# A list scheduler's delays, durations and engine hold replaced by measured ones: sliding-window attention and a two-layer expert on one Trainium2 core

## Chip, core and metric

One core of one Trainium2 chip. The metric is device time in microseconds (us) of one execution; the median of runs is given. Engines: PE is TensorE, DVE is VectorE, ACT is ScalarE, POOL is GpSimd, SP is SyncE (here it issues nearly all DMAs).

## The reference

Sliding-window attention over 8 sequences of 576 tokens with 8 heads of 64, then a two-layer network with a squared ReLU over all 4608 tokens:

```python
scores = scale * np.matmul(q, k.transpose(0, 1, 3, 2))        # q, k, v: (8, 8, 576, 64)
mask = np.abs(pos[:, None] - pos[None, :]) <= 32
attn = softmax(np.where(mask, scores, -1e9))
x = (attn @ v).transpose(0, 2, 1, 3).reshape(4608, 512)
h = np.maximum(x @ w_in, 0.0)                                 # w_in: (512, 2048)
out = (s * (h * h) + b) @ w_out                               # w_out: (2048, 512), out float32
```

Inputs and output are float32; the kernel multiplies in bfloat16.

## The kernel before

**A graph and a planner.** The kernel does not write its instructions in order. It calls `add` (L95) for each task: the engine ("stream"), the instructions, a cost in ns, the tiles read and written, and a key, which is a due time. `plan` (L126) then plays all engines forward: each engine has a time from which it is free, each task a time from which its inputs are ready, and the task that can start first is taken next, ties going to the lower key (L191 to L208). `release` (L175) sets when a user of a finished task is ready: its end, plus 100 ns for a DMA, 60 ns on the same engine, or the producer's `LAT` (L86), and 250 ns of `MARGIN` (L87) more where the user is PE. DMA rings have a model of their own (`serve`, `space`). `emit` (L234) writes each engine's tasks in the planned order with semaphore waits. On the chip every engine executes its own list strictly in order; so the plan's times decide nothing but the order, and where that order is wrong an engine waits in front of one task while a later one could run.

**Opening (sequence 0).** Q and K are loaded by pairs of heads, cast to bfloat16, transposed on PE (L704), evicted (L709 ACT for Q, L710 DVE for K), multiplied into scores (L943, into banks opened by L961), and passed through the exponential (L986 ACT). V is loaded by rows, cast (L602), placed by matmuls (L620) and evicted (L629, L630). Then each of five units is done: attention times V in 64-row tiles of PE (L868), reciprocal (L892) and product (L894) on DVE, a transpose on PE (L901) and a copy on ACT (L909) into the expert's input `xt`. The rest of sequence 0 beyond 512 tokens goes through L719 and L972.

**Expert.** The first layer (`s1`, matmuls L1123) works on a block of tokens (224, 128, 160, 256, 256, then 512 each) and a group of the 16 hidden tiles, into one of two banks `W`; ACT takes the ReLU (L1130), DVE squares (L1132). The second layer (`s2`, L1141; for the first three blocks `early`, L1172) accumulates 16 matmuls of 512 columns into a bank; DVE scales and adds (L1157), SP stores. Weights are loaded in eight pieces a layer and cast on POOL (L556). The pieces of the second layer hold their users back in the plan by `HELD` (L38) in place of `LAT`. `colsum` (L1182 to L1191) forms the column sums of the second weight.

**Later sequences.** Sequence 1 is turned on PE as sequence 0 is; from sequence 2 on, K and Q are cast on POOL (L759), transposed by DMA, and K is rearranged on POOL (L776). A unit there is one PE task (`pe_part`, L923): the first half of attention times V (L868), the scores of another unit (L810), and the second half, all in 64-row tiles between full-array matmuls. Its cost in the plan is a constant `SWITCH` plus 230 for scores plus 340 for attention times V. Exponential (L838 ACT) and mask (L842 DVE) follow, and V is cast on DVE (L590). Keys: the opening's PE tasks have keys from -99 to -21, the first blocks of the expert from -20 on, sequence 1 from -17.5 on.

Of the kernel before, what the change touches and what calls it, by code (L numbers as in the profile page):

```python
# [41 lines left out]
SWITCH = 215.0  # L42
# [23 lines left out]
class _Task:  # L66
    __slots__ = ("n", "stream", "fns", "cost", "lat", "key", "deps", "users", "left",
                 "ready", "start", "fin", "dma", "sem", "seq", "val", "used", "snap", "slack", "after", "next", "half", "mark")

    def __init__(self, n, stream, fns, cost, lat, key, dma, slack, after):  # L70
        self.slack, self.after, self.next = slack, after, []
        self.n, self.stream, self.fns, self.cost, self.lat, self.key, self.dma = \
            n, stream, fns, cost, lat, key, dma
        self.deps, self.users = set(), []
        self.ready = self.start = self.fin = 0.0
        self.sem = self.seq = self.val = None
        self.used = False
        self.snap = self.half = self.mark = None


class _Graph:
# [4 lines left out]
    LAT = {"pe": 260.0, "act": 130.0, "dve": 110.0, "pool": 150.0, "sp": 60.0}  # L86
    MARGIN = 250.0  # L87
# [7 lines left out]
    def add(self, stream, fns, cost, reads=(), writes=(), key=0.0, accum=False, dma=None, waits=(),  # L95
            lat=None, slack=0.0):
        if not isinstance(fns, list):
            fns = [fns]
        after = [self.chain] if key < -100 and self.chain else []
        t = _Task(len(self.tasks), stream, fns, cost, self.LAT[stream] if lat is None else lat, key,  # L100
                  dma, slack, after)
# [4 lines left out]
        for r in reads:  # L106
            assert r in self.writer, r
            t.deps.add(self.writer[r])
        for w in writes:
# [16 lines left out]
    def plan(self):  # L126

        free = {s: 600.0 for s in self.STREAMS}
# [7 lines left out]
        order = []  # L136
        rings, clock, room = {"sp": [], "act": []}, [0.0], {}
# [37 lines left out]
        def release(t):  # L175
            for u in t.users:
                u.left -= 1
                if u.stream == "pe" and t.stream == "pe":
                    r = t.fin
                elif t.dma is not None:  # L180
                    r = t.fin + 100.0 + u.slack
                elif u.stream == t.stream:
                    r = t.fin + 60.0
                else:
                    r = t.fin + t.lat + (self.MARGIN if u.stream == "pe" else 0.0)
# [4 lines left out]
        while len(order) < len(self.tasks):  # L190
# [19 lines left out]
            t.start = st  # L210
            free[t.stream] = t.fin = st + t.cost
# [114 lines left out]
def bass_sliding_window_symmetric__then__act_starrelu_kernel(  # L326
# [23 lines left out]
    with ExitStack() as es:  # L350
# [191 lines left out]
        def load_weights(which, i, x, key, eng):  # L542
# [6 lines left out]
            else:  # L549
# [7 lines left out]
                {"act": 1040.0, "dve": 690.0, "pool": 1100.0}[eng], reads=[("STG", si)], writes=[("W" + which, i, x)],  # L557
                key=key + 150.0, slack=100.0, lat=HELD[i] if which == "out" else None)
# [12 lines left out]
        def load_v(c, u, key, eng, waits=()):  # L571
# [6 lines left out]
            else:  # L578
# [5 lines left out]
                (650.0 if eng == "sp" else 500.0) * len(at), writes=[("VST", vs)], key=key, dma=("l", n // 2, (20.0, 17.0, 23.0)[min(c, 2)]), waits=waits)  # L584
            land["v", c, u] = g.tasks[-1]

        def cast_v(c, u, key, eng, slack):
# [3 lines left out]
                {"act": 617.0, "dve": 420.0, "pool": 750.0}[eng],  # L591
# [3 lines left out]
        def load_rows(y, load_key):  # L595
# [8 lines left out]
                {"dve": 650.0, "pool": 1180.0}[ROWE[y]], reads=[("VS", y)], writes=[("VN", y)], key=-28.0 + y, slack=200.0)  # L604
# [8 lines left out]
        def place_v():  # L613

            grid = PICK.rearrange("p a r -> p (a r)")
            def place(us, ys, key):
# [8 lines left out]
                    60.0 + 110.0 * nh, reads=[("VN", y) for y in ys] + ["PICK"], writes=[(name, x) for _, name, x in at],  # L625
                    key=key, slack=300.0)
                for u, (bank, name, x) in zip(us, at):
# [3 lines left out]
                        {"act": 190 + 0.833 * 64 * nh, "dve": 60 + 1.04 * 64 * nh}[EV0[u]], reads=[(name, x)],  # L631
# [53 lines left out]
        def cast_qk(stg, reads, eng, key, slack, swap):  # L685
# [6 lines left out]
                {"act": 620.0, "dve": 400.0, "pool": 640.0}[eng], reads=reads, writes=[("NAT", ni)],  # L692
# [3 lines left out]
        def turn_pair(b, name, pr, key, banks, eng, slack):  # L696
# [8 lines left out]
                       for i in range(ROWS)], 240.0, reads=[("NAT", ni), "IDENT"], writes=[res], key=key)  # L705
# [3 lines left out]
            add(*(("act", lambda e: e.copy(dst, order), 190 + 0.833 * BODY) if name == "q" and (b, pr) not in TURN_DVE else  # L709
                  ("dve", lambda e: e.tensor_copy(dst, order), 60 + 1.04 * BODY)), reads=[res],  # L710
                writes=[({"q": "QT", "k": "KT"}[name], slot, x, pr) for x in range(BODY // 64)], key=key)

        def turn_rest(b, key, banks):
# [6 lines left out]
                       for pr in range(NPAIR)], 240.0, reads=[("NAT", ni), "IDENT"], writes=[res], key=key)  # L720
            last = BODY // 64
            both = view.rearrange("p a (s x) -> p a x s", x=2)
            for name, dst, src in (("QT", QT[slot][:, :, WIN + BODY:WIN + S], both[:, :, 0, :]),
# [3 lines left out]
                    (lambda e, dst=dst, src=src: e.tensor_copy(dst, src)), {"dve": 60 + 1.04 * 256, "act": 190 + 0.833 * 256}[eng],  # L727
# [11 lines left out]
        def piece(b, parts, key, waits):  # L739
# [16 lines left out]
                dma=("l", sum(n for _, _, n, _ in parts) // 8, 74.0 if late(b) == "sp" else 61.0))  # L756
            for x in (0, 1):
# [4 lines left out]
                    110 + (0.53 if eng == "dve" else 1.05) * 1024, reads=stgr, writes=[("NAT", ni + x)], key=key + CASTS, slack=SLACK[0])  # L762
            for name, t0, n, p0 in parts:
# [10 lines left out]
                for c in range(t0, t0 + n, 128):  # L774
# [4 lines left out]
                        100 + 5.5 * w, reads=[("KTR", slot, t0)],  # L779
# [28 lines left out]
        def qk_part(c, u):  # L808
# [15 lines left out]
            return fns, reads, [("SC", hp) for hp in (0, 1)], 230.0  # L824

        def exp_mask(c, u, key=None, hps=((0, 1),)):
# [3 lines left out]
            for hs in hps:  # L830
# [5 lines left out]
                else:  # L836
                    flat_src, flat_dst = src, dst
                add("act", lambda e, dst=flat_dst, src=flat_src: e.activation(dst, src, AF.Exp, bias=0.0, scale=0.125),  # L838
                    190 + 0.833 * 512 * len(hs), reads=[("SC", hp) for hp in hs],
# [3 lines left out]
                    130 + 0.53 * 512 * len(hs), reads=[("E", ei, hp, pr) for hp in hs for pr in range(NPAIR)] + [("MASK", mi, p0) for p0 in (0, 64)],  # L843
# [6 lines left out]
        def av_part(b, u):  # L850
# [31 lines left out]
            return fns, reads, res, 340.0  # L882

        def finish(b, u, key=None):
# [12 lines left out]
                680, reads=avr + [("REC", ri)], writes=[("XN", xi)], key=key)  # L897
            x0 = b * S + r0
            if n < XPE:
# [3 lines left out]
                    for pr in range(NPAIR)], 230, reads=[("XN", xi), "IDENT"], writes=avr, key=key)  # L903
# [4 lines left out]
                for a0, a1 in zip(cuts, cuts[1:]):  # L908
                    add("act", lambda e, a0=a0, a1=a1: e.copy(  # L909
                        XT[:, :, a0 % XR:a0 % XR + a1 - a0], view[:, :, p0 + a0 - x0:p0 + a1 - x0]),  # L910
                        190 + 0.833 * 4 * (a1 - a0), reads=avr, writes=xt_res(a0, a1), key=key)
# [11 lines left out]
        def pe_part(key, av=None, sc=None, waits=()):  # L923
# [6 lines left out]
            t = add("pe", fns, SWITCH + sum(p[3] for p in parts) + (0.0 if sc else 150.0),  # L930
# [543 lines left out]
```

## Time and profile before

| | |
|---|---|
| median of 3 runs | 313.94 us (313.73 to 314.08) |
| span of the profiled execution, first to last instruction | 310.6 us |
| granted TensorE clock | 1.000 |
| PE matmuls busy | 295.3 us |
| first layer's matmuls, L1123 | 138.2 us |
| second layer's, L1141 | 120.6 us |
| attention times V from sequence 1 on, L868 into `avn` | 19.9 us |
| POOL, last work | before 220 us |

An instruction's row in order of time gives its start, its length, engine, line, operation, output and input, how many are merged, and, in brackets, how long the engine was idle before it and what ended that. The length of a matmul includes its way through the array, so the lengths of neighbours overlap. A row by stage gives the stretch, its length, then the busy time and number of instructions of PE, PE's weight loads, DVE, ACT and POOL, the granted clock, the share of the DMA engines and GB/s.

### The profile page before, as it was taken

Reading aid. Unit: us, or ns where it says so; the run is one execution under the profiler, and the core shown is the slowest. Engines: PE = TensorE matmul, PEld = TensorE weight load, DVE = VectorE, ACT = ScalarE, POOL = GpSimd, SP = SyncE. Lnnn points to the kernel's source line nnn. Section 1 sums busy time; section 2 is a strip of 40 time slices with the busy share of each in tenths; the row PEclk is TensorE's granted clock in tenths of the full one; section 3 lists DMA queues with packets and bytes.
Section 4 is the critical chain, followed back from the end, with each engine's and each line's share of the span. In section 5 each row is a group of like instructions: output and inputs, shape, how many; then the busy total and the mean of one; then the engine's idle time right before and its main releaser. Section 6 shows DMA issues by size and latency. Waiting matters only on the chain.

```text
span 310.6 us, 7883 instructions
## 1 busy us (share of the span) xinstructions
PE 295.3 (95%) x3305; PEld 160.3 (52%) x3348; DVE 191.8 (62%) x372; ACT 142.3 (46%) x224; POOL 106.8 (34%) x125
## 2 busy tenths in 40 slices
PE   7789999999999999999999999999999999999996
PEld 3469754577654454454444444444444444444444
DVE  4675587776677796886379658866655543333312
ACT  4757445256536673763156326635444333333300
POOL 6364786752526366261435331615000000000000
PEclk9999999999999999999999999999999999999999
DMA  7999999998997998899799799978211111000122
GB/s 223 333 384 372 371 268 235 245 168 271 247 192 210 282 184 192 287 145 154 215 291 151 139 262 281 141 146 203 80 53 53 51 46 36 34 34 35 37 96 77
DMA packets 100054, 56.09 MB, mean 181 GB/s; under 512 B 72048, under 2 KB 91248, under 8 KB 100016
## 3 DMA queue, kind: packets, MB, share of 16 engines
q1 hardware_dynamic: 100016, 55.56, 75.3%
q8 instruction: 27, 0.44, 0.6%
q14 instruction: 11, 0.09, 0.1%
HBM read 36.70 MB, written 9.44 MB: 149 GB/s over the span
## 4 chain that ended last, share of the span: by engine, by line
PE 78%; DMA 12%; SPq 3%; issue 2%; POOL 2%; DVE 2%; ACT 0%; POOLq 0%
PE o L1141 35%; PE w L1123 32%; DMA stg<-in_moe_w_out_dram 5%; PE avn L868 4%; DMA stg<-in_moe_w_in_dram 3%; DMA stg<-in_k_dram 3%; PE sc L810 2%; PE avn L1172 2%; DMA stg<-in_v_dram 1%; DVE gt L1132 1%; SPq L666 1%; PE o L1172 1%; POOL wout L556 1%; SPq L677 1%; PE avn L901 1%
## 5 line engine op out<-in xcount | busy, mean ns | idle before, releaser
L1123 PE MATMUL w<-xt,win 128*128 128x512 bf16 (+4 forms) x750 | 138.2, 325 | 2.9 <-ACT r L1130 1.6
L1130 ACT ACTIVATE r<-w 128x512 bf16<-128x512 f32 (+2 forms) x148 | 86.7, 586 | 100.1 <-PE w L1123 84.9
L1132 DVE TENSOR_TENSOR gt<-r 128x512 bf16<-128x512 bf16 (+2 forms) x148 | 87.1, 601 | 69.2 <-ACT r L1130 68.5
L1141 PE MATMUL o<-wout,gt 128*128 128x512 bf16 (+1 forms) x508 | 120.6, 372 | 2.4 <-issue 1.6
L1123 PEld LDWEIGHTS w<-xt,win 128*128 128x128 bf16 x768 | 68.1, 98 | 52.9 <-ACT r L1130 1.2
L1141 PEld LDWEIGHTS o<-wout,gt 128*128 128x128 bf16 x528 | 50.5, 98 | 55.1 <-DVE gt L1132 0.7
L759 POOL CAST nat<-stg 128x1024 bf16<-128x1024 f32 (+1 forms) x36 | 41.1, 1140 | 51.2 <-DMA stg<-in_q_dram 38.2
L776 POOL COPY kt<-ktr 128x512 bf16<-128x512 bf16 (+1 forms) x30 | 30.8, 1028 | 36.0 <-DMA ktr<-nat 34.5
L838 ACT ACTIVATE ex<-sc 128x1024 bf16<-128x1024 f32 (+1 forms) x28 | 28.7, 1023 | 24.4 <-PE avn L868 23.3
L1157 DVE SCALAR_TENSOR_TENSOR outs<-o,sb,cvec 128x512 f32<-128x512 f32 (+1 forms) x35 | 25.5, 732 | 18.9 <-PE o L1141 18.7
L894 DVE TENSOR_TENSOR xn<-avn,rec 128x512 bf16<-128x512 f32 (+1 forms) x31 | 21.4, 690 | 0.9
L842 DVE TENSOR_TENSOR ex<-ex,mask 128x1024 bf16<-128x1024 bf16 (+1 forms) x28 | 19.8, 708 | 1.2 <-ACT ex L838 0.5
L868 PE MATMUL avn<-vb,ex 64*64 64x65 bf16 x944 | 19.9, 197 | 0.3
L868 PEld LDWEIGHTS avn<-vb,ex 64*64 64x64 bf16 x944 | 12.9, 106 | 13.2 <-issue 5.5
L590 DVE CAST vb<-vst 128x512 bf16<-128x512 f32 (+1 forms) x28 | 12.3, 445 | 1.1 <-DMA vst<-in_v_dram 1.1
L892 DVE RECIPROCAL rec<-avn 128x8 f32<-128x8 f32 (+1 forms) x31 | 6.3, 202 | 8.7 <-PE avn L868 8.7
L810 PE MATMUL sc<-qt,kt 64*64 64x128 bf16 x432 | 11.3, 216 | 0.0
L909 ACT COPY xt<-avn 128x512 bf16<-128x512 bf16 (+2 forms) x14 | 7.1, 517 | 9.0 <-PE avn L901 9.0
L556 POOL CAST wout<-stg 128x1024 bf16<-128x1024 f32 x8 | 8.7, 1087 | 5.9 <-DMA stg<-in_moe_w_out_dram 5.7
L556 POOL CAST win<-stg 128x1024 bf16<-128x1024 f32 x8 | 8.4, 1055 | 3.3 <-DMA stg<-in_moe_w_in_dram 3.2
L1172 PE MATMUL o<-wout,gt 128*128 128x512 bf16 x28 | 8.2, 379 | 0.7 <-POOL wout L556 0.5
L986 ACT ACTIVATE ex<-sc 128x1024 bf16<-128x1024 f32 (+2 forms) x7 | 6.2, 902 | 5.0 <-PE sc L943 5.0
(118 smaller groups left out, 140.5 us busy)
## 6 DMA issues: line engine op xcount, KB each, us to landing
out_dram<-outs SPq DMA_DIRECT2D x35, 256.0 KB, 2.5
vst<-in_v_dram SPq DMA_DIRECT2D x28, 256.0 KB, 6.1
stg<-in_k_dram SPq DMA_DIRECT2D x6, 1024.0 KB, 10.4
stg<-in_q_dram SPq DMA_DIRECT2D x6, 1024.0 KB, 5.8
stg<-in_moe_w_in_dram SPq DMA_DIRECT2D x8, 512.0 KB, 8.8
stg<-in_moe_w_out_dram SPq DMA_DIRECT2D x8, 512.0 KB, 7.2
stg<-in_q_dram SPq DMA_DIRECT2D x8, 256.0 KB, 5.2
stg<-in_k_dram SPq DMA_DIRECT2D x8, 256.0 KB, 5.4
```

Source lines behind the costliest of these rows:

```text
L556: add(eng, (lambda e: e.copy(dst, stg)) if eng == "act" else (lambda e: e.tensor_copy(dst, stg)), {"act": 1040.0, "dve": 690.0, "pool": 11 ...
L759: add(eng, lambda e, x=x: e.tensor_copy(nat[0:top, 1024 * x:1024 * x + 1024].rearrange("p (i h d) -> p h i d", h=H, i=2), stg[0:top, :].re ...
L776: add("pool", lambda e, c=c, w=w: e.tensor_copy(KT[slot][:, :, c:c + w].rearrange("p a (s i) -> p a s i", i=4), KTR[slot][:, :, :, c // 4: ...
L838: add("act", lambda e, dst=flat_dst, src=flat_src: e.activation(dst, src, AF.Exp, bias=0.0, scale=0.125), 190 + 0.833 * 512 * len(hs), rea ...
L842: add("dve", lambda e, flat=flat, mask=mask: e.tensor_tensor(flat, flat, mask, ALU.mult), 130 + 0.53 * 512 * len(hs), reads=[("E", ei, hp, ...
L868: return [lambda e: e.matmul(av[64 * x:64 * x + 64, h, 0:D + 1], lhsT=buf[64 * g:64 * g + 64, h % 2, h // 2, c:c + 64], rhs=VB[64 * g:64 * ...
L894: add("dve", lambda e: e.tensor_tensor(XN[xi][0:p1, :].rearrange("p (a c) -> p a c", a=H), av[0:p1, :, 0:D], REC[ri][0:p1, :].rearrange("p ...
L1123: add("pe", [lambda e, g=g, kc=kc: e.matmul(wt[:, g, :], lhsT=WIN_BF[:, kc, (f0 + g) * 128:(f0 + g + 1) * 128], rhs=XT[:, kc, t0 % XR:t0 % ...
L1130: add("act", lambda e: e.activation(rt, wt, AF.Relu, bias=0.0, scale=1.0), 190 + 0.833 * ng * nt, reads=[("W", wb)], writes=[("R1", rb)], ...
L1132: add("dve", lambda e: e.tensor_tensor(GT[gs][:, f0:f0 + ng, g0:g0 + nt], rt, rt, ALU.mult), 130 + 0.53 * ng * nt, reads=[("R1", rb)], wri ...
L1141: add("pe", [lambda e, fc=fc: e.matmul(O[:, ob, 0:cn], lhsT=GT[gs][:, fc, g0:g0 + 128], rhs=WOUT_BF[:, fc, c0:c0 + cn], start=(fc == 0), s ...
L1157: add("dve", lambda e: e.scalar_tensor_tensor(OUTS[us][:, 0:cn], bank, SB128[:, 0:1], CVEC[:, c0:c0 + cn], ALU.mult, ALU.add), 200 + 1.07 ...
```

## The change

No instruction is added or removed, and the keys and the orders given by hand stay; the planner gets other numbers and four new rules. `LAT` becomes a table by producer and consumer. An engine may be free before its task has ended (`OVER`: ACT 100 ns and DVE 80 ns before, POOL 62 ns after). A PE task of another form ("64", "row", "column", or full) than the one before costs 92 ns more (`TURNED`), and `SWITCH` goes. DVE tasks of the form "two" and POOL's tasks hold each other up: one that starts while the other engine's is planned to run ends no sooner than that one's end plus its own cost less 130 ns. The margin of PE's inputs applies to keys over -20.05 alone (`FROM`). A reader of a PSUM bank depends on readers of that bank on other engines. Engines begin at 600 (PE, SP), 2000 (ACT), 900 (DVE) and 1100 ns (POOL) in place of 600 each. Costs of some forty calls move by up to some hundred ns.

```diff
-    LAT = {"pe": 260.0, "act": 130.0, "dve": 110.0, "pool": 150.0, "sp": 60.0}
-    MARGIN = 250.0
+    BANKS = ("W", "O", "SC", "AVN")
+    LAT = {"pe": {"act": 210.0, "dve": 210.0, "pool": 210.0, "sp": 210.0},
+           "act": {"pe": 55.0, "act": 0.0, "dve": 35.0, "pool": 35.0, "sp": 40.0},
+           "dve": {"pe": 60.0, "act": 12.0, "dve": 0.0, "pool": 35.0, "sp": 40.0},
+           "pool": {"pe": 55.0, "act": 35.0, "dve": 35.0, "pool": 62.0, "sp": 40.0},
+           "sp": {"pe": 60.0, "act": 60.0, "dve": 60.0, "pool": 60.0, "sp": 0.0}}
+    OVER = {"pe": 0.0, "act": 100.0, "dve": 80.0, "pool": -62.0, "sp": 0.0}
+    TURNED = 92.0
+    MARGIN, FROM = 250.0, -20.05
...
         for r in reads:
             assert r in self.writer, r
             t.deps.add(self.writer[r])
+            if r[0] in self.BANKS and not isinstance(r, str):
+                t.deps.update(x for x in self.readers.get(r, ()) if x.stream != stream)
...
-        free = {s: 600.0 for s in self.STREAMS}
+        free = {"pe": 600.0, "act": 2000.0, "dve": 900.0, "pool": 1100.0, "sp": 600.0}
...
-                if u.stream == "pe" and t.stream == "pe":
+                if t.dma is not None:
+                    r = t.fin + 40.0 + u.slack
+                elif u.stream == "pe" and t.stream == "pe":
                     r = t.fin
-                elif t.dma is not None:
-                    r = t.fin + 100.0 + u.slack
-                elif u.stream == t.stream:
-                    r = t.fin + 60.0
                 else:
-                    r = t.fin + t.lat + (self.MARGIN if u.stream == "pe" else 0.0)
+                    r = t.fin + self.LAT[t.stream][u.stream] + t.lat
+                    if u.stream == "pe" and u.key > self.FROM:
+                        r += self.MARGIN
...
-            t.start = st
-            free[t.stream] = t.fin = st + t.cost
+            t.start, t.fin = st, st + t.cost
+            if t.stream == "pe":
+                t.fin += self.TURNED if (t.form or "full") != shape else 0.0
+                shape = t.form or "full"
+            elif t.form == "two" or (t.stream == "pool" and t.dma is None):
+                mine, other = ("dve", "pool") if t.stream == "dve" else ("pool", "dve")
+                if st < pair[other]:
+                    t.fin = max(t.fin, pair[other] + t.cost - 130.0)
+                pair[mine] = t.fin
+            free[t.stream] = t.fin - self.OVER[t.stream]
...
-                {"act": 1040.0, "dve": 690.0, "pool": 1100.0}[eng], reads=[("STG", si)], writes=[("W" + which, i, x)],
-                key=key + 150.0, slack=100.0, lat=HELD[i] if which == "out" else None)
+                {"act": 1020.0, "dve": 670.0, "pool": 1042.0}[eng], reads=[("STG", si)], writes=[("W" + which, i, x)], form="two",
+                key=key + 150.0, slack=100.0, late=HELD[i] - 150.0 if which == "out" else 0.0)
...
-                        100 + 5.5 * w, reads=[("KTR", slot, t0)],
+                        250 + 6.4 * w, reads=[("KTR", slot, t0)],
...
-            return fns, reads, [("SC", hp) for hp in (0, 1)], 230.0
+            return fns, reads, [("SC", hp) for hp in (0, 1)], 221.0
...
-            return fns, reads, res, 340.0
+            return fns, reads, res, 303.0
...
-            t = add("pe", fns, SWITCH + sum(p[3] for p in parts) + (0.0 if sc else 150.0),
+            t = add("pe", fns, sum(p[3] for p in parts) + (20.0 if av and sc else 130.0 if av else 10.0), form="64",
...
-                130 + 0.53 * ng * nt, reads=[("R1", rb)],
+                155 + 0.53 * ng * nt, form="two", reads=[("R1", rb)],
```

DMA costs in the plan go from 23 to 21 (V from sequence 2 on), 74 to 66 (Q and K from sequence 2 on) and 86 to 82 (the stores). A PE task with scores alone costs 10 more than its matmuls; one with attention times V alone 130, one with both 20, where `SWITCH` was 215 (and 150 more without scores).

## The prediction

> **What bounds the kernel now.** I read the page's head first, then the busy time by stage, then the instructions in order of time wherever TensorE (PE) is idle, and last the unit that repeats.
>
> ```profile
> span 310.6 us, 7883 instructions
> ...
> PE 295.3 (95%) x3305; PEld 160.3 (52%) x3348; DVE 191.8 (62%) x372; ACT 142.3 (46%) x224; POOL 106.8 (34%) x125
> ...
> PE   7789999999999999999999999999999999999996
> ```
>
> PE is busy 95% and full in every slice but the first three and the last. The same by stage (time, then busy us of PE, its weight loads, DVE, ACT, POOL):
>
> ```profile
> 0.00:24.00 24.00, 18.98 (x339) 11.52 (x340) 14.57 (x40) 13.98 (x24) 13.65 (x29) 1.00 0.97 316
> 24.00:60.00 36.00, 34.09 (x499) 23.49 (x502) 25.14 (x50) 17.54 (x31) 25.47 (x34) 1.00 1.10 305
> 60.00:220.00 160.00, 155.70 (x1914) 83.74 (x1943) 117.48 (x212) 83.45 (x126) 67.72 (x63) 1.00 0.99 206
> 220.00:300.00 80.00, 79.09 (x512) 36.73 (x518) 32.11 (x69) 27.35 (x44) 0.00 (x0) 1.00 0.15 48
> 300.00:310.60 10.60, 7.47 (x50) 4.78 (x49) 2.47 (x4) 0.00 (x0) 0.00 (x0) 1.00 0.22 77
> ```
>
> PE's idle time is 24.00 - 18.98 = 5.0 us, then 1.9, 4.3, 0.9 and 3.1: 15.3 us in all. The last 3.1 is the last result's eviction and store behind the last matmul, and no order changes it. The change issues the same instructions, so PE's work is the same. What an order can win is idle time before the tail, mostly before 60 us; what it can lose is a wait of PE where there is none now.
>
> **The change, part by part.** It removes and adds no instruction. The new dependence between readers of one PSUM bank on different engines adds nothing that I find in the code: each bank is read between two writes by ACT alone or by DVE alone. What differs is the order on each engine and, with it, which waits are issued. So each part is priced by where PE waits now, and whether the new order keeps that wait.
>
> *1. No margin for the attention of sequence 0.* PE inputs with a key up to -20.05 lose the 250 ns margin, and their delays fall too: from DVE by 110 - 60 = 50, from ACT by 75, from POOL by 95 ns. In the first 14 us I find nothing to win: the first attention-times-V matmuls (L868) need the V rows, whose second half DVE casts from 12.92, when the load lands, to 13.62, and whose last eviction begins at 14.78. Scores that come earlier wait for that. I take 0, with -0.2 to +0.4: the longest wait of PE in the opening of banks is about 0.6 us (L961), and half of it either way seems a fair bound. After it:
>
> ```profile
> 14.78 0.69 DVE L630 CAST vb<-sc 128x512 bf16<-128x512 f32 x1
> ...
> 15.44 0.60 PE L961 MATMUL avn<-neg,ident 128*128 128x512 bf16 x2
> ...
> 15.88 0.39 PE L719 MATMUL w<-ident,nat 128*128 128x128 bf16 x4
> ...
> 16.20 0.72 PE L868 MATMUL sc<-vb,ex 64*64 64x65 bf16 x32
> ...
> 18.91 0.59 ACT L909 COPY xt<-sc 128x512 bf16<-128x512 bf16 x1
> ...
> 19.55 0.72 PE L868 MATMUL sc<-vb,ex 64*64 64x65 bf16 x32 [0.55 <-ACT xt L909]
> ```
>
> Unit 1's matmuls at 16.20 write the bank that DVE clears at 14.78 + 0.69 = 15.47. With 60 ns for the signal they could run at 15.53; the plan, adding 110 + 250 ns, put L961 and L719 ahead. They are 16.20 - 15.53 = 0.67 us late, and so is the chain behind them: reciprocal, product, transpose, ACT's copy at 18.91 (which then stood behind a 1.03 us exponential), and the wait of 0.55 us at 19.55. Without the margin the order is unit 1 first; the copy can pass the exponential, the 0.55 us wait goes, and 0.1 of the tail of that chain (the next attention work at 21.30) with it. I take -0.65; the bounds are 0 (L961 and L719, moved behind, delay sequence 0's last unit by as much) and -1.0.
>
> *2. The weights of the second layer.* PE waits twice for POOL's casts between 24 and 60 us:
>
> ```profile
> 32.28 0.38 PE L1172 MATMUL o<-wout,gt 128*128 128x512 bf16 x1 [0.48 <-POOL wout L556]
> ...
> 44.48 1.08 PE L1182 MATMUL avn<-wout,onesw 128*32 128x128 bf16 x64 [0.53 <-POOL wout L556]
> ```
>
> Behind the first stands a first-layer matmul (32.50) whose bank ACT freed at 30.94 + 0.44 = 31.38: it could have filled the gap. These two waits are a plan too early on the DMA. The change moves the same plan earlier still: 1100 - 1042 = 58 ns less cast, 60 ns less after landing, 95 ns less in the held delay (HELD - 150 + 55), 213 ns for each of eight casts. Against it, the opening is planned shorter by several margins of 300 to 350 ns in a row, so more first-layer work is placed ahead of L1172. Half of the first wait goes, -0.25; the second stays. Bounds: -1.0 (both gone) and +1.7 (each of the eight casts waited for 0.213 us longer).
>
> *3. Is the gain kept up to the dense part?* It is if sequence 1's attention is in time when PE comes earlier.
>
> ```profile
> 57.66 0.59 ACT L909 COPY xt<-w 128x512 bf16<-128x512 bf16 x1 [0.61 <-PE w L901]
> ...
> 58.33 1.03 PE L1172 MATMUL avn<-wout,gt 128*128 128x512 bf16 x4
> ...
> 59.93 1.92 PE L1123 MATMUL w<-xt,win 128*128 128x256 bf16 x16
> ```
>
> The input of block 3 is ready at 57.66 + 0.59 = 58.25, and PE takes it at 59.93, after L1172 and another unit. The cover is 59.93 - 58.25 = 1.7 us; 0.9 us pass through it. Without the cover, what PE gained would come back as a wait here. Price: 0.
>
> *4. Measured costs and the hold of DVE and POOL, from 60 us on.* PE keeps a 250 ns margin there, and its total for an input of ACT falls from 380 to 305 ns, DVE 360 to 310, POOL 400 to 305. The idle time there is not of waits: of 4.3 us most stands at the turn between 64-row and full matmuls.
>
> ```profile
> 84.47 1.03 PE L1141 MATMUL o<-wout,gt 128*128 128x512 bf16 x4
> ...
> 85.82 0.32 PE L868 MATMUL avn<-vb,ex 64*64 64x65 bf16 x16
> 86.30 1.03 PE L1141 MATMUL o<-wout,gt 128*128 128x512 bf16 x4 [0.16 <-issue]
> ```
>
> Full matmuls are 0.216 us apart (37 of them take 7.99 us at 292.80), so the four of 84.47 end at 85.33 and the unit takes 86.30 - 85.33 = 0.97 us. The old plan counts 215 + 230 + 340 = 785 ns, the new one 221 + 303 + 20 + 2 x 92 = 728: here it moves away from the chip, by 57 ns a unit. A plan with PE too fast makes PE late, which costs no wait of PE. Price 0; bounds -1.3 (below) and +1.5, which is about ten new waits as long as the ten of 0.16 us that PE now has for ACT.
>
> A rule bears on this last row: the Trainium skill, "TensorEngine Tiling (Array Packing)", Key Properties, says that a change of tiling mode drains TensorE. The row agrees in kind, with 0.16 us of "issue" and a unit longer than its matmuls; by that rule only fewer turns would save anything, and the new plan charges turns without avoiding them.
>
> **The sum.** -0.65 - 0.25 = -0.9 us: a span of 309.7 after 310.6. The median of 313.94 lies 3.3 us above the span, for what is around it, so **313.0 us**. A measurement here tells about 0.2%, 0.63 us, from no change.
>
> **The rivals.**
>
> *No change, 313.9.* The wait at 19.55 goes, but PE then meets the weights of 30 to 45 us that much earlier: they are set by DMA (its share is 1.04 to 1.11 in each ten of 10 to 50 us), and the gain is waited away. For it: both waits of part 2 are for that DMA. Against it: first-layer work was free at 31.4. Chance 0.16.
>
> *Slower: L1172 and the column sums queue ahead of their weights, 315.3.* PE runs in order; the 213 ns are taken off all eight casts, and where L1172 is placed that much earlier, everything behind it on PE waits. Eight times 0.213 is 1.7; less 0.3 us of part 1 that survives it, +1.4. It decides from five casts on, since 5 x 0.213 = 1.07 exceeds the 0.9 won. For it: the two waits exist already, with the longer delays. Chance 0.21.
>
> *Slower: sequence 1 or 2 is late, 315.0.* POOL is busy 8.2 of the 10 us from 50 to 60 and DVE 8.9 from 40 to 50. If the new order puts two POOL casts of 1.14 us ahead of the casts of V or q that block 3 needs, its input moves from 58.25 by 2.3 us, and PE, coming 0.5 us earlier, waits about 2.3 + 0.5 - 1.7 = 1.1 us at the end of its filling. The other orders (keys, order of weights, pacing) are left as they stood for the old delays, so such a swap is not excluded. Chance 0.15.
>
> *Faster by more, 311.5.* Both weight waits go (-1.0), the opening wins 0.2 and 0.65, and one or two units come to stand side by side, so that two turns fall out at 0.97 - 0.54 = 0.43 us for the pair of turns round a unit (0.54 is the new plan's 221 + 303 + 20 for the matmuls): about -2.5. For it: of the 1.9 us idle from 24 to 60, PE's waits for POOL and DVE are 1.2. Against it: several must go right. Chance 0.14.
>
> **Chances and range.** The forecast has 0.34, so faster by over 0.2% is 0.34 + 0.14 = 0.48, the same 0.16, slower 0.21 + 0.15 = 0.36. The range takes in both signs: below, the larger gain with one turn more (0.43) gives 311.1; above, the 1.7 us of part 2 and 0.7 of the late sequence give 316.3. The forecast alone would stand between 312.3 and 313.4.
>
> **What would show it.** Right: unit 1's L868 ahead of L961 and L719 and near 15.5, no wait for ACT near 19.5, under 4.5 us idle in the first 24 us, L1172's first wait shorter, idle time from 60 to 300 us near 5.2. Wrong: longer waits of PE for POOL's casts at 30 to 45 us, a wait for ACT or DVE at 56 to 62 us, or new waits of PE among the units after 60 us.

## The result and the profile after

The changed kernel took 318.33 us in the median (315.06 to 322.06) where the kernel before took 313.73 beside it: the ratio is 1.0101, 95% interval [1.0079, 1.0124]. It is slower by 1.0%, some 3.2 us. The medians here and below are of all executions of a kernel, while the ratios leave out those more than 1.5% above the kernel's fastest (four of the changed kernel's eleven, one of before's), so that a ratio can differ from the quotient of two medians, which is 1.0147 here. The profiled execution has a span of 314.9 us after 310.6. Its page, head and busy time of PE in 40 slices:

```profile
span 314.9 us, 7884 instructions
...
PE 296.9 (94%) x3306; PEld 160.2 (51%) x3348; DVE 185.1 (59%) x372; ACT 141.5 (45%) x224; POOL 107.6 (34%) x125
...
PE   7789997999999999999999699999999999999996
```

PE's work is the same, the span 4.3 us longer, and two slices behind the first three, the seventh (47 to 55 us) and the twenty-third (173 to 181 us), are thinner than before. By stage (stretch, length, busy us of PE, its weight loads, DVE, ACT, POOL, granted clock, DMA share, GB/s):

```profile
0.00:24.00 24.00, 19.19 (x326) 10.46 (x327) 13.39 (x39) 13.35 (x22) 12.67 (x29) 1.00 0.93 297
24.00:60.00 36.00, 33.66 (x474) 23.68 (x478) 23.99 (x48) 18.29 (x33) 25.43 (x34) 1.00 1.01 301
60.00:220.00 160.00, 153.35 (x1903) 82.34 (x1931) 110.71 (x210) 80.35 (x123) 69.52 (x64) 1.00 1.03 208
220.00:300.00 80.00, 78.93 (x555) 37.02 (x557) 33.77 (x73) 29.48 (x47) 0.00 (x0) 1.00 0.14 46
```

PE's idle time was 5.0, 1.9, 4.3 and 0.9 us and is 4.8, 2.3, 6.65 and 1.1: the stage from 60 to 220 us has lost most, 2.35 us (some 28 matmul records are missing there in both traces, by the counts of matmuls and weight loads, so the difference stands). What PE waited for longest (engine, tile, line, released by; us in total, times, longest):

```profile
PE avn L885 <- POOL kt L793: 2.8, 1, 2.8
...
PE w L736 <- POOL nat L708: 1.4, 1, 1.4
```

The first is one wait, for a K that POOL rearranges (L793, formerly L776); from 60 us on PE had waited for no K before. In order of time on PE, then on POOL:

```profile
175.20 1.03 PE L1158 MATMUL o<-wout,gt 128*128 128x512 bf16 x4
179.06 0.32 PE L885 MATMUL avn<-vb,ex 64*64 64x65 bf16 x16 [2.84 <-POOL kt L793]
...
179.94 3.40 PE L1158 MATMUL o<-wout,gt 128*128 128x512 bf16 x15 [0.16 <-issue]
```

```profile
177.98 4.80 POOL L793 COPY kt<-ktr 128x512 bf16<-128x512 bf16 x4 [7.09 <-DMA ktr<-nat]
```

PE stood in front of the unit from 176.2; the first K copy ended at 179.0. Behind the unit on PE's list stood sixteen second-layer matmuls, 3.4 us of work, which ran without a wait as soon as the unit was past (the row has 15 of them, but 16 weight loads: one matmul record is missing, and its place is the 0.16 us of "issue"). The same unit and copies in the kernel before:

```profile
180.83 0.32 PE L868 MATMUL avn<-vb,ex 64*64 64x65 bf16 x16
```

```profile
176.00 5.24 POOL L776 COPY kt<-ktr 128x512 bf16<-128x512 bf16 x5 [6.92 <-DMA ktr<-nat]
```

There the copies began at 176.00, and the unit came at 180.83, 3.8 us behind the end of the first: K is 1.9 us later now, the unit was put 4.6 us earlier.

### The profile page after: what moved, and what is told of

It reads as the page before. It is cut to its first block, busy times and chain, and to the rows that moved or that the text cites. A ratio compares the mean times of both kernels' runs of the same rounds, so it can differ in the third digit from the quotient of the medians.

```text
span 314.9 us, 7884 instructions
## 1 busy us (share of the span) xinstructions
PE 296.9 (94%) x3306; PEld 160.2 (51%) x3348; DVE 185.1 (59%) x372; ACT 141.5 (45%) x224; POOL 107.6 (34%) x125
## 4 chain that ended last, share of the span: by engine, by line
PE 69%; DMA 19%; SPq 4%; POOL 3%; issue 2%; DVE 1%; ACT 1%; POOLq 0%
PE o L1158 31%; PE w L1140 28%; DMA stg<-in_k_dram 5%; DMA vst<-in_v_dram 4%; DMA stg<-in_moe_w_in_dram 3%; PE avn L885 3%; DMA stg<-in_moe_w_out_dram 2%; DMA ktr<-nat 2%; POOL nat L776 2%; DMA stg<-in_q_dram 2%; PE sc L827 2%; PE avn L1189 2%; SPq L683 1%; SPq L694 1%; SPq L598 1%
## 5 line engine op out<-in xcount | busy, mean ns | idle before, releaser
L1149 DVE TENSOR_TENSOR gt<-r 128x512 bf16<-128x512 bf16 (+2 forms) x148 | 78.9, 541 | 78.2 <-ACT r L1147 77.9
L1158 PE MATMUL o<-wout,gt 128*128 128x512 bf16 (+1 forms) x515 | 123.6, 373 | 1.1 <-issue 0.5
L1140 PEld LDWEIGHTS w<-xt,win 128*128 128x128 bf16 x768 | 67.4, 98 | 53.4 <-ACT r L1147 1.9
L776 POOL CAST nat<-stg 128x1024 bf16<-128x1024 f32 (+1 forms) x36 | 40.6, 1127 | 49.4 <-DMA stg<-in_q_dram 35.9
L793 POOL COPY kt<-ktr 128x512 bf16<-128x512 bf16 (+1 forms) x30 | 32.0, 1067 | 34.6 <-DMA ktr<-nat 33.2
L859 DVE TENSOR_TENSOR ex<-ex,mask 128x1024 bf16<-128x1024 bf16 (+1 forms) x28 | 21.3, 762 | 3.7 <-ACT ex L855 2.4
L1189 PE MATMUL avn<-wout,gt 128*128 128x512 bf16 x30 | 8.3, 380 | 0.1
```

What stands on the lines that cost most here:

```text
L776: add(eng, lambda e, x=x: e.tensor_copy(nat[0:top, 1024 * x:1024 * x + 1024].rearrange("p (i h d) -> p h i d", h=H, i=2), stg[0:top, :].re ...
L793: add("pool", lambda e, c=c, w=w: e.tensor_copy(KT[slot][:, :, c:c + w].rearrange("p a (s i) -> p a s i", i=4), KTR[slot][:, :, :, c // 4: ...
L859: add("dve", lambda e, flat=flat, mask=mask: e.tensor_tensor(flat, flat, mask, ALU.mult), 155 + 0.53 * 512 * len(hs), form="two", reads=[( ...
L1140: add("pe", [lambda e, g=g, kc=kc: e.matmul(wt[:, g, :], lhsT=WIN_BF[:, kc, (f0 + g) * 128:(f0 + g + 1) * 128], rhs=XT[:, kc, t0 % XR:t0 % ...
L1149: add("dve", lambda e: e.tensor_tensor(GT[gs][:, f0:f0 + ng, g0:g0 + nt], rt, rt, ALU.mult), 155 + 0.53 * ng * nt, form="two", reads=[("R1 ...
L1158: add("pe", [lambda e, fc=fc: e.matmul(O[:, ob, 0:cn], lhsT=GT[gs][:, fc, g0:g0 + 128], rhs=WOUT_BF[:, fc, c0:c0 + cn], start=(fc == 0), s ...
```

## The experiments

"Ratio" is against the kernel before on the same chip.

**Where the loss lies.** Three kernels splice the two planned orders, without a change of any instruction:

```diff
+        g.order = [g.tasks[i] for i in ORDER]
```

`h1_first` has the changed order up to the first L1123 (about 20 us) and before's behind it, `h4_open` up to the first layer's work on block 3 (about 60 us); `h3_rest` the reverse, before's order up to there and the changed one behind.

> The changed order up to the first matmul of the expert alone (about 20 us), the order of the kernel before behind it. The prediction gave this part -0.65 us. If that holds, the time is 0.3 to 1 us under the kernel before; if the opening without margin costs, it is over it by 0.5 us or more, or its granted clock is lower.

> The changed order up to the first layer of block 3, the order of the kernel before behind it. Theory A: the time is within 1 us of the kernel before, no wait over 0.6 us after 60 us. Theory B: 315 or more, with waits before 60 us and a granted clock under 0.995 in half of the runs.

> The order of the kernel before up to the first layer of block 3 (about 60 us), the changed order behind it. Theory A (the loss is after 60 us, where the changed plan has no slack left for late DMAs): PE waits over 2 us in all for K, V or the product behind V between 60 and 215 us, and the time is 315.5 or more. Theory B (the loss is in the opening: waits and a lower granted clock before 60 us): the time is within 1 us of the kernel before and the clock 0.995 or more.

`h1_first`: 314.28 us, ratio 1.0017 [0.9995, 1.0039]. `h4_open`: 313.56, 1.0011 [0.9987, 1.0035]. `h3_rest`: 318.11, 1.0104 [1.0058, 1.015], as much as the whole change. The opening's order neither wins nor loses anything that these ratios show (they reach 0.4% at most); the loss is made behind 60 us. The waits of PE in `h3_rest`:

```profile
PE avn L942 <- POOL kt L850: 3.6, 2, 3.3
```

It is the same wait for K, near 176 us.

**The DMA times in the plan.** `b1_dma` is the kernel before with the changed DMA times alone, `e1_dma` the changed kernel with before's:

```diff
-                    r = t.fin + 100.0 + u.slack
+                    r = t.fin + 40.0 + u.slack
...
-  ... dma=("l", n // 2, (20.0, 17.0, 23.0)[min(c, 2)]), waits=waits)
+  ... dma=("l", n // 2, (20.0, 17.0, 21.0)[min(c, 2)]), waits=waits)
...
-  ... 74.0 if late(b) == "sp" else 61.0))
+  ... 66.0 if late(b) == "sp" else 61.0))
...
-  ... dma=("o", 8, 86.0 * cn / DM + 4), key=key)
+  ... dma=("o", 8, 82.0 * cn / DM + 4), key=key)
```

> The kernel before with only the new planner's costs of DMAs (66, 21 and 82, 40 ns after landing). Theory 1: the first unit of the sequence near 176 us comes 9 us of PE's work earlier, PE waits 1 to 4 us for K, and the time rises by 1 to 4 us over the kernel before, to 315 to 318. Theory 2: no wait over 0.5 us after 60 us, time within 0.7 us of the kernel before.

> The changed kernel with the old planner's costs of DMAs (74, 23 and 86 again, 100 ns after landing in place of 40), all else as changed. Theory 1 (the plan counts on K too early, because its DMAs became cheaper): PE's wait of 2.8 us for the rearranged K near 176 us is gone, since the first unit of that sequence moves behind some 6 us more of PE's work; the time falls by 2 to 3 us, to about 313.5. Theory 2 (leaner delays and margins of PE's inputs place the unit too early): the wait stays over 2 us and the time stays within 1 us of 316.

`b1_dma`: 319.96 us, 1.0173 [1.0128, 1.0219]. These four numbers alone cost more than the whole change. Its waits behind 60 us:

```profile
PE avn L901 <- DVE xn L894: 3.1, 2, 2.4
PE avn L868 <- POOL kt L776: 2.4, 3, 1.7
```

`e1_dma`: 319.09, 1.0182 [1.015, 1.0213]. The wait for K is gone, as it should be, but the time is not won. PE now waits near 97 us, for a block's input:

```profile
97.61 0.40 PE L918 MATMUL avn<-ident,xn 128*128 128x128 bf16 x4 [1.25 <-DVE xn L911]
98.91 2.32 PE L1140 MATMUL w<-xt,win 128*128 128x512 bf16 x10 [0.90 <-ACT xt L926]
```

This plan has the old DMA times but the new, shorter delays, and there the chain attention, normalization, transpose, copy into `xt` comes too late for PE. That the DMA times are the only cause falls with this run.

**More room for the DMAs.** `m2_slack` is the changed kernel with more slack for the users of loads:

```diff
-SLACK = (1000.0, 2000.0, 3000.0, 3000.0)
+SLACK = (2500.0, 4500.0, 3000.0, 6000.0)
```

> The changed kernel with more slack behind DMAs in the plan and nothing else: casts of Q and K 2500 ns after landing (1000), K's rearrangement 4500 (2000), casts of V 6000 (3000). Theory A: the waits after 60 us fall below 1.5 us in all and the time by 2 us or more against the changed kernel, to 313.5 to 316. If slack is not what is missing, waits and time stay.

317.23 us, 1.0106 [1.006, 1.0151]: no wait for K any more and nothing won. In order of time on POOL, DVE and PE:

```profile
67.78 5.61 POOL L793 COPY kt<-ktr 128x512 bf16<-128x512 bf16 x5 [3.95 <-DMA ktr<-nat]
68.00 1.29 DVE L607 CAST vb<-vst 128x512 bf16<-128x512 f32 x1
...
72.61 0.34 PE L918 MATMUL avn<-ident,xn 96*128 96x96 bf16 x4 [1.18 <-DVE xn L911]
...
73.93 0.41 DVE L607 CAST vb<-vst 128x512 bf16<-128x512 f32 x1
```

K is copied in time now, but a cast of DVE's beside the copies takes 1.29 us, three times the 0.41 us of one behind them, and the product that PE waits for is late.

**The delays and the margin.** `b4_lat` is before with the new table of delays and no margin up to -20.05; `b2_from` before with only the latter; `e2_margin` the changed kernel with before's delays and its margin everywhere; `e5_from` the changed kernel with the margin in the opening too.

```diff
(b4_lat; b2_from has the condition on the key alone)
-                    r = t.fin + t.lat + (self.MARGIN if u.stream == "pe" else 0.0)
+                    r = t.fin + self.PAIR[t.stream][u.stream] + t.lat
+                    if u.stream == "pe" and u.key > -20.05:
+                        r += self.MARGIN
(e2_margin)
-                    r = t.fin + self.LAT[t.stream][u.stream] + t.lat
-                    if u.stream == "pe" and u.key > self.FROM:
-                        r += self.MARGIN
+                    r = t.fin + self.OLD[t.stream] + t.lat + (self.MARGIN if u.stream == "pe" else 0.0)
(e5_from)
-    MARGIN, FROM = 250.0, -20.05
+    MARGIN, FROM = 250.0, -1000.0
```

> The kernel before with the new table of delays and the margin only over -20.05, with the old costs of tasks and DMAs and without the hold. If the lean delays are a part of the loss on their own (the changed kernel with the old delays was 1.005 in place of 1.010), it is slower than before by 1 to 3 us with waits of PE for K or for the product behind V; if only the DMA costs lose, it is within 1 us.

> The kernel before without the 250 ns margin for keys up to -20.05, nothing else; the order behind about 60 us stays as it is. The prediction's part 1 gives -0.65 us: 312.3 to 312.9 against 313.2. If the opening's order has no such effect, the time is within 0.5 us of the kernel before; unit 1's product with V stands ahead of L961 and L719 if the prediction's reading of the order holds.

> The changed kernel with the old delays (260, 130, 110, 150, 60 ns on the same engine) and the 250 ns margin for every input of PE, all else as changed. Theory 2: the wait near 176 us goes and the time falls to about 313.5. Theory 1: a wait for K of 1 us or more stays and the time stays at 315 or more.

> The changed kernel with the margin of 250 ns for all of PE's inputs, the opening's too. If the missing margin in the opening costs (theory 3: PE queues in front of late inputs in the first 24 us), PE's idle time there falls below the 4.8 us of the changed kernel and the time by over 0.5 us. Theory 1: the time stays within 1 us of the changed kernel, 315 to 317.

`b4_lat`: 315.76 us, 1.0051 [1.0025, 1.0078]. `b2_from`: 314.35, 1.0016 [0.9989, 1.0043]. `e2_margin`: 315.76, 1.0054 [1.0024, 1.0084], with waits for K of 1.7 us at the longest and 4.4 us in all, in an execution 2.5 us above its median. `e5_from`: 317.7, 1.0127 [1.0083, 1.017]. `b4_lat`, with the shorter delays and the opening's missing margin, lies half a per cent over before, without a wait for K of more than 0.2 us; that is no more than some redraws below cost that should mean nothing, so it is not shown that the delays cost this. Taking the margin off the opening costs and wins nothing that can be seen.

**The hold.** `e4_hold` is the changed kernel whose plan knows no hold between DVE and POOL.

```diff
-                if st < pair[other]:
+                if False:
```

> The changed kernel without the hold between DVE and POOL in the plan (costs, delays and turns as changed); no task of POOL moves, 119 of PE's and of DVE's do. M: with the hold, which lengthens planned DVE and POOL tasks, gone, the plan is still earlier than the chip: 317 to 320 us, the wait for K near 176 us at 2.8 us or longer. S: other waits, 315 to 319 us. If the hold is what costs the time: 313.5 to 315 us.

315.42 us, 1.0057 [1.0026, 1.0088]. Not slower than the changed kernel, against the expectation for a plan that is too early, and not at before either. The wait for K is 1.2 us at the longest. By itself the run decides little.

**Both put back.** `e6_both` is the changed kernel with both before's DMA times (as in `e1_dma`) and before's delays and margin (as in `e2_margin`). The measured durations, the turns, the early ends and the hold stay.

> The changed kernel with before's DMA costs, its landing of 100 ns, its delays and its margin everywhere; the measured durations, the turns, the early ends and the hold stay. 169 of PE's 412 tasks stand elsewhere than before. If the lean DMA times and delays are the second half of the loss: no more than a neutral redraw costs, 0.2 to 0.7% over before (314.2 to 315.8 us), and no wait for K over 0.5 us near 176 us. If the durations, turns and hold themselves cost: 316.5 us or more.

313.41 us, ratio 0.9984 [0.9967, 1.0002]. The loss is gone, whole. PE's list at the place of the wait, and POOL's:

```profile
180.31 3.62 PE L1159 MATMUL o<-wout,gt 128*128 128x512 bf16 x16
183.85 0.32 PE L886 MATMUL avn<-vb,ex 64*64 64x65 bf16 x16
```

```profile
179.15 5.33 POOL L794 COPY kt<-ktr 128x512 bf16<-128x512 bf16 x5 [7.63 <-DMA ktr<-nat]
```

K comes 1.2 us later than in the changed kernel (179.15 after 177.98), and nobody waits: the unit stands behind sixteen second-layer matmuls, where the changed kernel has that many behind the unit, and comes 3.6 us after the first copy's end. The wait was one of order, not of a slower DMA.

**Does any redraw cost?** By then two theories were open: M, the changed numbers plan the work earlier than the chip does it; and S, before's order is a finely balanced draw, and any replanning loses. Six kernels redraw an order, five of them before's and `m4_m275` the changed one's. Five do it by a number that should mean little; `p3_dmaup` moves the DMA times the other way, by about as much as the change took off them:

```diff
(p1_margin)  -    MARGIN = 250.0                 +    MARGIN = 275.0
(p4_lat)     -    "act": 130.0, "dve": 110.0     +    "act": 135.0, "dve": 115.0
(p2_switch)  -SWITCH = 215.0                     +SWITCH = 235.0
(p6_lean)    -SWITCH = 215.0                     +SWITCH = 200.0
(p3_dmaup)   -DMA times 74, 23, 86               +DMA times 82, 25, 90
(m4_m275)    -MARGIN, FROM = 250.0, -20.05       +MARGIN, FROM = 275.0, -20.05
```

> The kernel before with the margin of PE's inputs at 275 ns in place of 250; 189 of PE's 412 tasks change place. M (the changed numbers plan too early): these numbers are more cautious, not less, so within 0.2% of before, 313.4 to 314.4 us, and no wait of PE over 1 us behind 60 us. S (any redraw of a finely balanced order loses): 315 to 317 us, as the run with dearer DMAs, with one or more new waits of 0.8 to 2 us behind 60 us, at places other than those of the changed kernel.

> The kernel before with the delays of ACT and DVE 5 ns longer (135 and 115); 206 of PE's 412 tasks change place. M: 313.4 to 314.4 us, no wait of PE over 1 us behind 60 us. S: 315 to 317 us with new waits behind 60 us.

> The kernel before with its constant for a unit raised from 215 to 235 ns: a planner as pessimistic as before, whose order differs from about 60 us on by up to 13 places. Theory P (the old planner's surplus of delays and costs is what keeps inputs early): time within 1 us of the kernel before. Theory S (the old order is one tuned draw, and another plan loses whatever its numbers): slower by 1 to 4 us, with waits over 0.5 us between 60 and 215 us.

> The kernel before with SWITCH at 200 ns in place of 215, so a PE planned faster by 15 ns a unit; 161 of PE's 412 tasks change place. If only the redraw counts: 0.2 to 0.7% over before, 314.2 to 315.8 us. If planning PE too fast costs by itself (the mirror of the run with 235, which was at +0.2%): 316 us or more, with waits of PE for xn, xt or K of 0.8 us or more behind 60 us. If it costs nothing, as the prediction had it: within 0.2% of before.

> The kernel before with its costs of later DMAs moved the other way, up by as much as the change takes off them: 82, 25 and 90 in place of 74, 23 and 86. Theory P: no slower than the kernel before by more than 1 us, no wait for K over 0.3 us. Theory S: slower by 1 to 4 us.

> The changed kernel with its margin at 275 ns in place of 250; 37 of PE's 412 tasks change place, by at most 3 places, and 2 of SP's. M: the DMAs' times in the plan are the same, so the wait for K near 176 us stays at 2.5 to 3.5 us and the time within 0.3% of the changed kernel, 316.5 to 318.5 us. S: the waits fall elsewhere, anything from 314 to 319 us.

`p1_margin`: 315.24 us, 1.0063 [1.0032, 1.0095]. `p4_lat`: 315.52, 1.0056 [1.0028, 1.0084]. `p2_switch`: 314.66, 1.0022 [0.9991, 1.0054]. `p6_lean`: 314.88, 1.0045 [1.0021, 1.0068]. `p3_dmaup`: 316.31, 1.0069 [1.0046, 1.0093]. `m4_m275`: 320.04, 1.0167 [1.0104, 1.023], with the wait for K at 3.2 us, as expected, and a time over the expected 316.5 to 318.5 us.

In `m4_m275` that wait costs more than itself. Right behind it the granted clock stands at 0.50 for 3.4 us, and sixteen second-layer matmuls take 5.31 us, where those of `e6_both` took 3.62:

```profile
179.37 0.32 PE L885 MATMUL avn<-vb,ex 64*64 64x65 bf16 x16 [3.20 <-POOL kt L793]
...
180.02 5.31 PE L1158 MATMUL o<-wout,gt 128*128 128x512 bf16 x16
```

```profile
176.00:180.00 4.00, 0.80 (x49) 0.59 (x48) 0.40 (x1) 0.00 (x0) 1.66 (x2) 1.00 0.39 78
180.00:184.00 4.00, 4.00 (x23) 1.49 (x12) 3.21 (x5) 1.02 (x1) 3.64 (x4) 0.59 1.09 272
```

The changed kernel's profiled execution kept its clock behind its wait of 2.84 us; whether its executions at a lower clock lost it there is not on record.

Five nanoseconds of planned delay cost 0.56%: M alone would have had that run at before's time, so a redraw has a price. But it does not fall where the change's does. Waits of PE and busy time of the dense stages of `p1_margin`:

```profile
PE avn L901 <- DVE xn L894: 0.4, 1, 0.4
...
60.00:220.00 160.00, 159.40 (x1973) 84.02 (x1972) 112.19 (x211) 83.73 (x127) 69.84 (x66) 1.00 0.99 207
220.00:300.00 80.00, 79.93 (x519) 36.82 (x518) 33.27 (x72) 28.11 (x46) 0.00 (x0) 1.00 0.14 45
```

PE has one wait there, of 0.4 us. Against S's expectation there are no new waits behind 60 us; what it lost is ahead of them, as at the weights (`p6_lean` waits 1.53 us for POOL at 32.72, before 0.48 at 32.28).

A count over each trace shows it. It takes the time at which PE starts an instruction less the work ahead of it in PE's list (each matmul at 0.417 us per 1000 columns, a quarter of it for 64-row tiles): what remains is PE's lost time up to there. Relative to before, in us, from one execution each, which is good to about 1 us:

| up to | 60 us | 80 us | 160 us | 200 us | 300 us |
|---|---|---|---|---|---|
| the changed kernel | 1.0 | 1.7 | 1.7 | 4.2 | 4.2 |
| `h3_rest` | 0.3 | 1.0 | 2.0 | 5.3 | 5.3 |
| `b1_dma` | 0.8 | 1.7 | 5.6 | 7.4 | 7.2 |
| `e1_dma` | 0.6 | 2.0 | 4.6 | 4.6 | 4.9 |
| `p1_margin` | 1.6 | 2.0 | 2.3 | 2.3 | 2.3 |
| `p4_lat` | 1.4 | 1.9 | 1.6 | 1.6 | 1.6 |
| `p2_switch` | 0.8 | 1.4 | 2.2 | 2.2 | 2.2 |
| `p6_lean` | 1.4 | 1.9 | 1.7 | 1.7 | 1.7 |
| `p3_dmaup` | 0.0 | 0.7 | 1.8 | 3.1 | 3.4 |
| `e6_both` | 0.7 | 2.5 | 1.8 | 2.2 | 2.2 |

(`e6_both`'s profiled execution was 1.4 us above its median.) With before's DMA times and (but for 5 ns) its delays, a redraw loses 1.4 to 2.5 us up to 80 us and no more than 0.8 behind them; with leaner ones the kernels of the table lose another 2.5 to 5.5 us there (`b4_lat` and `m2_slack`, by the same count, 1.6 and 1.7). `p3_dmaup`, with dearer DMAs, loses 2.7 us there too, in shorter waits (0.9 us for an exponential, 0.7 for `xt`): a plan can err on that side as well.

**How early the plans are.** The planner's own times, set beside the trace, for the first K copy that the unit near 180 us needs (us):

| | planned end of the copy | traced end | PE waits for this K |
|---|---|---|---|
| before | 183.3 | 177.1 | no |
| `p1_margin` | 181.4 | 178.2 | no |
| `e6_both` | 182.3 | 180.2 | no |
| `e1_dma` | 182.8 | 182.7 | no |
| `b1_dma` | 173.4 | 178.5 | yes |
| the changed kernel | 173.5 | 179.0 | 2.84 us |
| `m4_m275` | 173.6 | 179.3 | 3.2 us |

In this table the DMA times alone decide on which side of the trace the plan stands: with the old ones K came 0.1 to 6.2 us before its planned time, with the new ones more than 5 us behind it. In the changed kernel the DMA queue's rows begin and end this chain so:

```profile
154.30 0.39 SPq L768 DMA_DIRECT2D stg<-in_q_dram  x1
...
169.04 2.36 SPq L783 DMA_TRANSPOSE qt<-nat  x1
171.45 3.16 SPq L783 DMA_TRANSPOSE ktr<-nat  x1
...
175.92 1.22 SPq L783 DMA_TRANSPOSE ktr<-nat  x1
```

From the first load to the start of the last transpose are 21.6 us; its plan had 19.8 (149.3 to 169.1). In the kernel before the trace has 21.5 and the plan 21.7:

```profile
153.54 0.39 SPq L751 DMA_DIRECT2D stg<-in_q_dram  x1
...
175.03 1.23 SPq L766 DMA_TRANSPOSE ktr<-nat  x1
```

The old numbers fitted this stretch, the new ones are 1.8 us short in it, and 5.0 us had been lost before it began.

## Why the prediction was wrong

**Part 4 is the step that failed.** It put the measured costs from 60 us on at "Price 0", because "A plan with PE too fast makes PE late, which costs no wait of PE". That looks at PE against itself. The order is set by PE against the engines and queues that feed it, and part 4 priced the units' 57 ns and the delays only; the DMA times of the later sequences (23 to 21, 74 to 66, 86 to 82, landing 100 to 40), though listed in the change, were in no term of the sum (part 2 counted the 60 ns less after landing, but for the second layer's weights only). PE did come late: it reached the unit at 176.2, 2.4 us behind the planned 173.9. But K came 5.5 us late (173.5 planned, 179.0 traced), and the difference, less the 0.4 us that the plan had left between the two, is the wait of 2.84 us. The step cost 1.0% by `h3_rest`, about 3.3 us, over the bound of +1.5. Its sentence on PE alone is neither borne out nor refuted: `p6_lean`, which plans only PE faster, lost 0.45%, with no wait behind 60 us, and a meaningless redraw costs as much. What part 4 meant, measured durations and the hold, cost nothing in the one order that has them without the leaner numbers, `e6_both`.

**Part 4's row was misread.** The 0.97 us of a unit at 85.33 to 86.30 rests on a matmul record that is missing from the trace of before (3305 matmuls for 3348 weight loads). The trace of `p1_margin` has all 3348, and there a unit takes 0.75 us: four matmuls from 82.11 at 0.216 us end at 82.97, the next starts at 83.72.

```profile
82.11 1.03 PE L1141 MATMUL o<-wout,gt 128*128 128x512 bf16 x4
...
83.72 1.05 PE L1123 MATMUL w<-xt,win 128*128 128x256 bf16 x8
```

So the new plan's 728 ns were nearer than the old 785, not further. The waits of 0.16 us on "issue" and for ACT are the same gap in the records, and they are gone where the records are whole. In the trace of before waits of this length make up 4.6 of the 5.2 us that the prediction took for idle time of PE from 60 to 300 us, so next to none of it was idle. That the row agreed in kind with the Trainium skill's rule on tiling modes was no evidence.

**Part 1** had half of the mechanism and not the gain. In the changed kernel unit 1 passes L719, but not L961:

```profile
16.28 0.60 PE L978 MATMUL avn<-neg,ident 128*128 128x512 bf16 x2
16.81 0.72 PE L885 MATMUL sc<-vb,ex 64*64 64x65 bf16 x32
17.46 0.40 PE L736 MATMUL w<-ident,nat 128*128 128x128 bf16 x4
...
20.39 0.93 PE L1140 MATMUL w<-xt,win 128*128 128x224 bf16 x8 [0.54 <-POOL win L573]
```

It runs at 16.81, not at 15.53 and later than before's 16.20, and the 0.55 us wait for ACT has become one of 0.54 us for POOL's cast of the first layer's weights, one step later. -0.65 measured as nothing: `b2_from` 1.0016 [0.9989, 1.0043], `h1_first` 1.0017 [0.9995, 1.0039].

**Part 2**: both waits for the second layer's casts are gone, as its bound of -1.0 had it, and in their place PE waits 1.41 us for POOL's cast at 50.31. Together with part 1 the opening comes out even (`h4_open` 1.0011 [0.9987, 1.0035]), so -0.9 was not there, and **part 3** had nothing to keep. The new dependence between readers adds nothing, as said.

**The rivals.** "Sequence 1 or 2 is late" had the right kind of cause, an attention input too late for PE, but the wrong sequence and reason: it is a later one, near 176 us, and the order of PE's own list. The slower rival at the weights did not happen. The range's upper end, 316.3, was made of the opening's mishaps and lies 0.6 us below 313.73 x 1.0101 = 316.9.

**What stays open.** Leaner numbers for DMAs or delays alone leave 0.5 to 1.8%, and the parts don't add: undoing only the DMA times made the changed kernel slower. Of the ten kernels here whose plan has them behind 60 us, the changed one included, seven lie 1.0% or more over before and three at 0.5 to 0.6%; the six with before's numbers there, nearly before's or dearer ones lie between -0.2 and 0.7%. That the leaner numbers lose is shown by this and by the K wait; what each of them costs alone is not. Which wait a given plan runs into could not be told ahead. Nor is it shown why redraws of before's order cost 0.2 to 0.7% while `e6_both`, in which 169 of PE's 412 tasks stand elsewhere, costs nothing. That before's order is a lucky one among its neighbours is the likeliest reading, not a shown one.

## To carry to other kernels

In a planned order, the margin belongs where the cost of an error is lopsided: an input planned too late moves work in front of it, while one planned too early leaves an in-order engine standing. So before making a planner's numbers "true", set its times for the inputs that feed the bound engine beside the trace; if the trace is earlier now, that lead is a reserve that the change spends. And judge a planner's number against several redraws by meaningless amounts: here anything under 0.7% could have been that alone.

## What the runs showed of the hardware

**The clock of PE drops in steps.** The granted clock of an execution lies at 1.000, 0.994, 0.989, 0.984, 0.978 and so on, in steps of about 0.0054, that is 1.7 us of 314, or 3.4 us at half rate; in `e6_both` (0.993) the clock stands at 0.50 from 8.2 to 11.6 us and at 1.00 on both sides. Twice such a stretch lies behind 24 us: in `m4_m275` behind the wait of 3.20 us shown above, and in `b4_lat` at 44.0 us behind one of 2.15 us. In `e1_dma` it is in the opening, by stage:

```profile
12.00:16.00 4.00, 2.75 (x63) 1.55 (x64) 2.70 (x5) 2.39 (x6) 1.84 (x3) 0.92 1.17 308
16.00:20.00 4.00, 3.92 (x61) 2.11 (x60) 2.36 (x5) 1.15 (x4) 1.57 (x2) 0.50 1.05 389
20.00:24.00 4.00, 3.78 (x117) 2.88 (x115) 1.54 (x5) 2.60 (x4) 3.59 (x6) 0.72 1.06 388
```

The clock is at 0.50 from 16 to 20 us, behind a stretch in which PE had been idle for 1.25 of 4 us. Idle time alone does not tell it: in the changed kernel's profile PE is idle for 1.35 us of the same stretch, and the clock stays at 1.00. Before's executions beside the experiments lay at 0.998 or above four times in five, the changed kernel's in two of eleven; `p1_margin` took 314.3 to 314.8 us at 1.000 and 317.4 to 318.4 at 0.967 to 0.973. The opening's order has a part in it: `h1_first` and `h4_open` lie at 0.998 or above in four of twelve executions each, before beside them in 20 of 23. So a wait of PE can cost more than its own time, and this makes up part of the changed kernel's spread; but its two executions at 0.999 took 315.50 and 316.78 us, 1.8 and 3.1 us over before's median, so the clock is not the whole loss. The Trainium skill, "TensorE: Matmul & The Clock Gate", Part 1 (The HAM clock gate), has PE at half rate after an idle window of about 3.4 us, in windows that run free of the kernel; the size of the steps agrees, but the stretch ahead of the drop in `e1_dma` was not idle, with PE busy for 2.75 of 4 us.

**DVE beside POOL.** A cast of 128x512 takes DVE 0.41 us with POOL's copies past (73.93 in `m2_slack`) and 1.29 us while POOL copies K (68.00), whose copies take 5.61 / 5 = 1.12 us in the mean. The Trainium skill, "SBUF — State Buffer" (SBUF: two separate sides), says that DVE, in its two-port modes or with two inputs in SBUF, and GpSimd take a shared pair of ports for a whole instruction, and that the other waits; the 1.29 us fit a cast of 0.41 us behind the rest of one POOL copy. Here it means that a K copied earlier, beside DVE's work, makes that work late.
